# Two of eight directly transformed token tiles done by seven block products, with the weights' combinations prepared earlier

## The chip, the cores and the metric

The kernel runs on one core of one Trainium2 chip. The metric is device time in microseconds (us) of one execution. Differences of about 0.2% (1.3 us) are what a measurement of this kernel can tell from none.

## The reference, cut to what matters

```python
xn = _layernorm(x, axis=-1)                     # x: 2048 tokens x 512 channels
a = einsum("bsd,ed->bse", xn, dft_hid_re)       # DFT along the channels
b = einsum("bsd,ed->bse", xn, dft_hid_im)
s = einsum("ts,bse->bte", dft_seq_re, a) - einsum("ts,bse->bte", dft_seq_im, b)
y = _layernorm(xn)
g = silu(gelu(y @ w1 + b1) @ w2 + b2)
return x + s * g
```

The change concerns the first two products alone, the channel DFT.

## The kernel before

All matrices are float32. Each is split into a rounded high part (an fp32r copy made by ScalarE, ACT below) and a low part (value minus high part, made by VectorE, DVE below), and each product is made of three matmuls on TensorE (PE below): high x high, high x low, low x high. A matmul here takes a 128x128 stationary piece and 512 moving columns.

The program has four stages: the channel DFT (0 to 89 us of the profile), the first layer of the MLP, its second layer, and the sequence DFT. The 2048 tokens are 16 tiles of 128. In the first stage the tiles 0 to 7 are transformed directly: `dft_mm(i, m)` makes for tile i the real (m=0) or imaginary (m=1) result with 12 matmuls (4 pieces of channels, 3 terms), and `dft_out(i, m)` scales it out of PSUM on ACT and queues its store. Tiles 4 to 7 are the second token block; `xt_centre` takes the means off its two halves of channels `xtr[1, 0]` and `xtr[1, 1]` (tiles named xT), and `xt_make` splits them. Tiles 8 to 15 go by seven block products (Strassen's scheme in Winograd's form: two halves of channels, pairs of token tiles i and j, real and imaginary half of the result). `q_product(p)` makes product p for four pairs, six matmuls each. Its left sides are `W` (the DFT matrix itself, products 1, 2, 4) or the combinations that `a_sum`, `a_round` and `a_rest` make of it (A5, A6, A7, A3); its right sides are the halves 11, 21, 22 and the sums t1 to t4, made by `y_sum`, `y_round`, `y_rest` after `y_centre` (means) and `y_scale` (row factors). Products 1, 6, 7 and 4 accumulate in one PSUM bank (y), 5 and 3 in another (z), 2 in a third (x). Between them `q_after` reads the bank: for 1, 5, 6, 4 a scaled copy on ACT, for 2, 3, 7 a scaled addition on DVE.

Order is written out by hand: every engine executes its instructions in the order in which the code issues them, and waits on semaphores where an operand is not there or a place not free. `turn_n` and `turn_r` turn rows of means and factors (a transpose on PE, a copy rt on ACT, a store to DRAM from ACT's queue); `row_load` brings them back, spread over all partitions, through SP's queue (tiles rown and rowR). [...]

```python
    KEY_Q = {1: "y", 6: "y", 7: "y", 4: "y", 5: "z", 3: "z", 2: "x"}
```

Of the kernel before, what the change touches and what calls it, by code (L numbers as in the profile page):

```python
# [14 lines left out]
P = 128  # L15
# [5 lines left out]
def fnet_mixer_kernel(ctx: ExitStack, tc: tile.TileContext, x, xT, ct, wt, w1, w2, b1, b2, out):  # L21
# [153 lines left out]
    def rows_turn(key, copies=1):  # L175
        st = row_st[key]
        n = st.shape[1]
        ps = bank("rp" + key)
        nc.tensor.transpose(ps[:n, :P], st, ident)
        sb = small.tile([n, P], F32, tag="rt", bufs=1, name="rt" + key)  # L180
        nc.scalar.activation(sb, ps[:n, :P], AF.Copy)
        row_d[key] = dram.tile([copies, n * P], F32, name="rd" + key)
        nc.scalar.dma_start(out=row_d[key].rearrange("r (b p) -> b r p", p=P),
                            in_=sb[:, None, :].broadcast_to([n, copies, P]))
# [148 lines left out]
    def xt_centre(b, k2):  # L333
        nc.vector.tensor_sub(xtr[b, k2], xtr[b, k2], both(mrow[b]))

    def xt_make(b, k2):
        hi, lo = split_two(xtr[b, k2], f"xt{b}_{k2}")
        for k in range(2):
            for c in range(NC):
                xt[b * NC + c, 2 * k2 + k] = (hi[:, k, c * P:(c + 1) * P], lo[:, k, c * P:(c + 1) * P])  # L340

    weights = [None] * (2 * NK)

# [27 lines left out]
    def neg_means(b, n=NC):  # L371
        nc.vector.tensor_scalar(nm[:, NEG[b] * NC:NEG[b] * NC + n], mv1[:, b * NC:b * NC + n, 0], -1.0, None,
                                op0=ALU.mult)

    def act_stats(i):
        c = i % NC
        nc.scalar.activation(junk(0), xs[i], AF.Copy, scale=-1.0 / D, accum_out=nm[:, NC + c:NC + c + 1])
        nc.scalar.activation(junk(1), xs[i], AF.Square, bias=nm[:, NC + c:NC + c + 1], accum_out=sq[:, c:c + 1])
# [117 lines left out]
    dft_mm(2, 1)  # L496
    dft_out(2, 0)

    def xt_prepare(b):
        for k in range(NK // 2):  # L500
            xt_centre(b, k)
        for k in range(NK // 2):
            xt_make(b, k)


    w1_raw, w1_op = {}, {}

    def w1_load(j):
# [48 lines left out]
    def a_sum(p):  # L557
        a11, a12, a21, a22 = (room_w[m, k2] for m in range(2) for k2 in range(2))
        if p == 5:
            nc.vector.tensor_add(a22, a21, a22)  # L560
        if p == 7:
            nc.vector.tensor_sub(a21, a11, a21)
        if p == 6:
            nc.vector.tensor_sub(a11, a22, a11)
        if p == 3:
            nc.vector.tensor_sub(a12, a12, a11)
# [12 lines left out]
    RIGHT = {1: "11", 2: "21", 3: "22", 4: "t4", 5: "t1", 6: "t2", 7: "t3"}  # L579
    KEY_Q = {1: "y", 6: "y", 7: "y", 4: "y", 5: "z", 3: "z", 2: "x"}  # L580
    qx, q_part = {}, {}

    def q_place(name, c):
        if c % 2 == 0:
            q_part[name, c] = guest(f"q{name}_{c}")
        return q_part[name, c - c % 2][:, c % 2, :]


    def q_out(i, m, e):
# [1 line left out]
        while len(stores) > LAG:  # L591
            store()

    def q_after(p, c):
        i, j = 2 * NC + c, 3 * NC + c
        f, g = (qq[:, t - HB:t - HB + 1] for t in (i, j))
        nf, ng = (nq[:, t - HB:t - HB + 1] for t in (i, j))
        acc = qx[KEY_Q[p], c]
        if p in (1, 5, 6, 4):
            e = q_place(p, c)  # L600
            nc.scalar.activation(e, acc, AF.Copy, scale={1: f, 5: ng, 6: g, 4: nf}[p])
            if p == 4:
                q_out(i, 1, e)
        else:
            e = q_part[{2: 1, 3: 6, 7: 5}[p], c - c % 2][:, c % 2, :]
            nc.vector.scalar_tensor_tensor(e, acc, {2: f, 3: g, 7: ng}[p], e, op0=ALU.mult, op1=ALU.add)
            q_out(*{2: (i, 0), 3: (j, 0), 7: (j, 1)}[p], e)

    def q_mm(p, c):
        key = KEY_Q[p]  # L610
        yh, yl = y_op[RIGHT[p], 1]
        if p in (1, 5, 2):
            qx[key, c] = bank(f"q{key}{c}")
        cols = slice(c * P, (c + 1) * P)
        terms = [(a[:, k, cols], w) for k in range(2)
                 for a, w in ((yh, a_op[p][k][0]), (yh, a_op[p][k][1]), (yl, a_op[p][k][0]))]
        for n, (a, w) in enumerate(terms):
            nc.tensor.matmul(qx[key, c], a, w, start=p in (1, 5, 2) and n == 0,  # L618
                             stop=p in (2, 3, 4) and n == len(terms) - 1, skip_group_check=True)

    def q_product(p, *steps):
        for c in range(NC):
# [3 lines left out]
            for do in steps[c:c + 1]:  # L626
                for o in do:
                    o()

    def turn_n():  # L630
        row_st["n"] = nm
        rows_turn("n")
        mrow[2], mrow[3] = row_load("n", 2)

    def turn_r():
        row_st["R"] = rr[:, HB:3 * HB]
        rows_turn("R")

    for i in range(3, HB):
        if i == 3:  # L640
            xt_prepare(1)
            for q in (13, 14, 15):
                act_stats(q)
            for q in (10, 11):
                stats(mv1, xs[q], q)
            neg_means(2)
            neg_means(0, 2)
        if i == 4:
            factors = second_factors()
            a_sum(5)  # L650
            factors()
        if i == 5:
            a_sum(7)
            last_factors()
            a_sum(6)
            a_sum(3)
        if i == 6:
            for b in (2, 3):
                for k2 in range(2):
                    y_centre(b, k2)  # L660
        if i == 7:
            y_scale(0, 2)
            y_round("11", 1)
            y_scale(1, 2)
            y_round("21", 1)
            y_rest("11", 1)
            y_rest("21", 1)
        dft_mm(i, 0, {4: turn_r} if i == 5 else {})
        if i == 5:
            rrow = [None] * 2 + row_load("R", 2, 2)  # L670
        dft_out(i - 1, 1)
        dft_mm(i, 1, {3: turn_n} if i == 4 else {})
        dft_out(i, 0)
    dft_out(HB - 1, 1)

    for p, (m, k2) in {1: (0, 0), 2: (0, 1), 4: (1, 1)}.items():
        a_op[p] = [weights[m * NK + 2 * k2 + k] for k in range(2)]
# [4 lines left out]
    def then(f, *a):  # L682
        return lambda: f(*a)

    rrow[0:2] = row_load("R", 2)
    centred_load(0)
    y_scale(0, 3)
    a_round(5)
    y_sum("t1", 1)
    y_round("t1", 1)  # L690
    a_rest(5)
    y_rest("t1", 1)
    q_product(1, [then(y_scale, 1, 3), then(y_round, "22", 1)], [then(y_sum, "t2", 1)],
              [then(y_round, "t2", 1), then(y_rest, "22", 1)], [then(a_round, 6)])
    q_product(2, [post(2, 0), then(y_rest, "t2", 1)], [post(2, 1), then(a_rest, 6)],
              [post(2, 2), then(y_sum, "t3", 1), then(y_round, "t3", 1), then(a_round, 3)], [post(2, 3)])
    q_product(5, [then(a_rest, 3)], [then(y_rest, "t3", 1), then(y_sum, "t4", 1), then(a_round, 7)],
              [then(y_round, "t4", 1), then(a_rest, 7)], [then(y_rest, "t4", 1)])
    early.close()
    wr = early.enter_context(tc.tile_pool(name="wr", bufs=1, reuse_waits="tile"))  # L700
    wp = early.enter_context(tc.tile_pool(name="wp", bufs=4, reuse_waits="tile"))
# [454 lines left out]
    def factors(u, name):  # L1156
        q, n = units[u]
        lr = [[t[:, (n % 2) * W2 + k * P:(n % 2) * W2 + (k + 1) * P] for k in range(2)] for t in c_left[q, n // 2][name]]
        return lr, c_ops[u][name]
# [154 lines left out]
```

## Time and profile before

| | |
|---|---|
| median of 3 runs | 666.75 us (666.4 to 666.99) |
| profiled execution, its own time | 666.61 us |
| its span | 664.8 us |
| PE busy | 659.8 us (99%), 2920 matmuls |
| DVE busy | 538.9 us (81%) |
| ACT busy | 359.8 us (54%) |
| granted TensorE clock | 1.00 in every stretch |

The span runs from the first instruction to the last. The profiled execution's own time is 1.8 us more than its span and 0.14 us under the median.

### The profile page before, as it was taken

Reading aid. Unit: us, or ns where it says so; the run is one execution under the profiler, and the core shown is the slowest. Engines: PE = TensorE matmul, PEld = TensorE weight load, DVE = VectorE, ACT = ScalarE, POOL = GpSimd, SP = SyncE. Lnnn points to the kernel's source line nnn. Section 1 sums busy time; section 2 is a strip of 40 time slices with the busy share of each in tenths; the row PEclk is TensorE's granted clock in tenths of the full one; section 3 lists DMA queues with packets and bytes.
Section 4 is the critical chain, followed back from the end, with each engine's and each line's share of the span. In section 5 each row is a group of like instructions: output and inputs, shape, how many; then the busy total and the mean of one; then the engine's idle time right before and its main releaser. Section 6 shows DMA issues by size and latency. Waiting matters only on the chain.

```text
span 664.8 us, 8196 instructions
## 1 busy us (share of the span) xinstructions
PE 659.8 (99%) x2920; PEld 543.8 (82%) x2920; DVE 538.9 (81%) x570; ACT 359.8 (54%) x413; POOL 50.8 (8%) x84
## 2 busy tenths in 40 slices
PE   9999999999999999999999999999999999999997
PEld 5888888888888888888888888888888888888886
DVE  7789978866777866888979998739877299997986
ACT  6846557545456755555455544456444454646540
POOL 0002000321121100000000000000000001210100
PEclk9999999999999999999999999999999999999999
DMA  9889250887979999798699996416545558996984
GB/s 316 276 278 253 92 227 1 331 310 277 340 299 353 416 413 365 268 387 311 254 389 409 373 321 228 159 51 203 188 149 134 128 131 263 301 258 238 317 253 139
DMA packets 71877, 172.81 MB, mean 260 GB/s; under 512 B 6896, under 2 KB 22812, under 8 KB 71836
## 3 DMA queue, kind: packets, MB, share of 16 engines
q1 hardware_dynamic: 59488, 132.27, 56.6%
q0 software_dynamic: 12032, 39.86, 18.9%
q8 instruction: 23, 0.38, 0.2%
q10 hardware_dynamic: 316, 0.16, 0.1%
q14 instruction: 18, 0.15, 0.1%
HBM read 121.91 MB, written 50.35 MB: 259 GB/s over the span
## 4 chain that ended last, share of the span: by engine, by line
PE 99%; DVE 0%; issue 0%
PE pz L928 20%; PE px L928 18%; PE ma L928 11%; PE hy L743 11%; PE mb L928 9%; PE hz L743 6%; PE pd L397 5%; PE pw L928 5%; PE qy L618 3%; PE hx L743 3%; PE pd L409 2%; PE px L1249 2%; PE pw L1249 2%; PE qz L618 2%; PE qx L618 1%; PE idle_ps L202 1%
## 5 line engine op out<-in xcount | busy, mean ns | idle before, releaser
L1034 DVE TENSOR_TENSOR c<-c,c 128x1024 f32<-128x1024 f32 x32 | 39.0, 1217 | 4.2 <-DMA c<-ct 4.2
L81 DVE TENSOR_TENSOR w1l<-w1r,w1h 128x1792 fp32r<-128x1792 f32 x7 | 14.2, 2025 | 21.6 <-ACT w1h L521 21.6
L748 ACT ACTIVATE hc<-hc,b_t 128x1024 f32<-128x1024 f32 (+1 forms) x18 | 17.3, 961 | 25.0 <-DVE hc L788 22.6
L63 DVE TENSOR_TENSOR R_b1l<-c,R_b1h 128x1024 fp32r<-128x1024 f32 x16 | 19.4, 1220 | 12.9 <-ACT R_b1h L62 9.9
L62 ACT ACTIVATE R_s3h<-c 128x1024 fp32r<-128x1024 f32 x16 | 17.0, 1062 | 23.7 <-DVE c L1034 9.5
L928 PE MATMUL pw<-R_s1h,L 128*128 128x512 f32 x96 | 29.7, 389 | 0.0
L62 ACT ACTIVATE R_b2h<-c 128x1024 fp32r<-128x1024 f32 x16 | 16.9, 1057 | 21.2 <-DVE c L1039 15.0
L63 DVE TENSOR_TENSOR R_s2l<-c,R_s2h 128x1024 fp32r<-128x1024 f32 x16 | 19.5, 1220 | 8.6 <-PE pz L928 8.6
L62 ACT ACTIVATE R_s2h<-c 128x1024 fp32r<-128x1024 f32 x16 | 17.0, 1061 | 16.7 <-PE px L928 9.3
L62 ACT ACTIVATE R_s1h<-c 128x1024 fp32r<-128x1024 f32 x16 | 16.4, 1050 | 11.7 <-DVE c L1045 11.7
L63 DVE TENSOR_TENSOR R_s3l<-c,R_s3h 128x1024 fp32r<-128x1024 f32 x16 | 19.5, 1218 | 4.0 <-PE pz L928 4.0
L1042 POOL DMA_DIRECT2D c<-ct x8 | 7.0, 873 | 200.8 <-DVE c L1039 162.9
L62 ACT ACTIVATE R_b1h<-c 128x1024 fp32r<-128x1024 f32 x16 | 16.7, 1053 | 10.4 <-DMA c<-ct 4.4
L62 ACT ACTIVATE R_a1h<-c 128x1024 fp32r<-128x1024 f32 x16 | 16.9, 1054 | 8.9 <-PE pz L928 7.2
L928 PEld LDWEIGHTS pw<-R_s1h,L 128*128 128x128 f32 x96 | 18.0, 188 | 3.7
L63 DVE TENSOR_TENSOR R_b2l<-c,R_b2h 128x1024 fp32r<-128x1024 f32 x16 | 19.4, 1217 | 1.9 <-PE px L928 1.9
L63 DVE TENSOR_TENSOR R_a1l<-c,R_a1h 128x1024 fp32r<-128x1024 f32 x16 | 19.5, 1218 | 1.3 <-PE px L928 1.1
L62 ACT ACTIVATE R_s4h<-c 128x1024 fp32r<-128x1024 f32 x16 | 16.8, 1049 | 6.1 <-PE pz L928 3.3
L63 DVE TENSOR_TENSOR R_s4l<-c,R_s4h 128x1024 fp32r<-128x1024 f32 x16 | 19.5, 1218 | 0.7 <-PE px L928 0.7
L1039 DVE TENSOR_TENSOR c<-c,c 128x1024 f32<-128x1024 f32 x16 | 19.6, 1222 | 0.4
L62 ACT ACTIVATE w2h<-w 128x1024 fp32r<-128x1024 f32 (+1 forms) x14 | 13.2, 944 | 10.7 <-DVE w L856 3.9
L63 DVE TENSOR_TENSOR R_s1l<-c,R_s1h 128x1024 fp32r<-128x1024 f32 x16 | 18.8, 1219 | 0.1
(968 smaller groups left out, 2221.6 us busy)
## 6 DMA issues: line engine op xcount, KB each, us to landing
c<-ct SPq DMA_DIRECT2D x68, 512.0 KB, 5.6
m<-h_d SPq DMA_DIRECT2D x48, 512.0 KB, 7.0
h_d<-ht POOLq DMA_DIRECT2D x21, 512.0 KB, 7.0
s_d<-sa SPq DMA_DIRECT2D x32, 256.0 KB, 4.0
la<-s_d SPq DMA_DIRECT2D x32, 256.0 KB, 6.7
h_d<-hc POOLq DMA_DIRECT2D x13, 512.0 KB, 3.8
x<-x SPq DMA_DIRECT2D x16, 256.0 KB, 5.2
sa<-a_d SPq DMA_DIRECT2D x8, 512.0 KB, 5.8
```

What stands on the lines that cost most here:

```text
L62: nc.scalar.activation(hi, src, AF.Copy)
L63: nc.vector.tensor_sub(lo, src, hi.bitcast(F32))
L81: nc.vector.tensor_sub(hi_lo[1], src, hi_lo[0].bitcast(F32))
L397: nc.tensor.matmul(acc, xt[i, k][px], weights[m * NK + k][pw], start=n == 0, stop=n == len(terms) - 1)
L409: nc.tensor.matmul(dacc[i, m], xt[i, k][px], weights[m * NK + k][pw], start=seen[i, m] == 0, stop=seen[i, m] == 3 * NK - 1)
L618: nc.tensor.matmul(qx[key, c], a, w, start=p in (1, 5, 2) and n == 0, stop=p in (2, 3, 4) and n == len(terms) - 1, skip_group_check=True)
L743: nc.tensor.matmul(acc[:, tau, :], w[:, W1_AT[p], k * P:(k + 1) * P], r[:, k, :], start=p in (1, 5, 2) and i == 0, stop=p in (2, 3, 4) and ...
L748: nc.scalar.activation(dst, src, AF.Gelu_apprx_tanh, bias=b1_t[:, row:row + 1])
L928: nc.tensor.matmul(acc[k][:, tau, :], a, c[:, tau, :], start=first and i == 0, stop=last and i == len(terms) - 1, skip_group_check=True)
L1034: nc.vector.tensor_sub(t, t, raw)
L1039: nc.vector.tensor_add(raw, raw, t)
L1249: nc.tensor.matmul(acc[KEY[name]][k][:, tau, cols], a[k], c[:, tau, cols], start=False, stop=last and u == us[-1] and i == 2, skip_group_c ...
```

## The change

Tiles 6 and 7, the last two of the second token block, no longer go through `dft_mm`. They become one pair of the seven block products, taken on the centred columns, with results scaled by the row factors `rr` and `nr1` (`tau` = "u"). Tiles 4 and 5 stay direct; `xt_round` splits their columns only. Sums t1 to t4, high and low parts of the pair are 2x128 columns wide. `a_sum`, `a_round` and `a_rest` move ahead of the products of the pair; means and factors of tiles 8 to 15 (`y_centre`, `y_scale`) move behind them, between the products. The turned rows get two places (rt) in place of one.

```diff
-        sb = small.tile([n, P], F32, tag="rt", bufs=1, name="rt" + key)
+        sb = small.tile([n, P], F32, tag="rt", bufs=2, name="rt" + key)
...
+    PAIRS = 1
+    CONV = NC - 2 * PAIRS
+    half_ops = {}
+
+    def xt_round(b, k2):
+        n = CONV * P
+        if k2 == 0:
+            half_ops[b] = operand(f"xt{b}h"), operand(f"xt{b}l")
+        hi, lo = (t[:, :, k2 * n:(k2 + 1) * n] for t in half_ops[b])
...
+        nc.scalar.activation(hi, xtr[b, k2][:, :, :n], AF.Copy)
+        return lambda: nc.vector.tensor_sub(lo, xtr[b, k2][:, :, :n], hi.bitcast(F32))
...
     def y_round(name, tau):
+        if tau == "u":
+            y_op[name, tau] = u_place(name)
+            nc.scalar.activation(y_op[name, tau][0], y_raw[name, tau], AF.Copy)
+            return
...
+    def q_scale(tau, t):
+        if tau == 1:
+            return qq[:, t - HB:t - HB + 1], nq[:, t - HB:t - HB + 1]
+        return rr[:, t:t + 1], nr1[:, t:t + 1]
...
+    def u_product(p):
+        for c in range(PAIRS):
+            q_mm(p, c, "u")
+            if p in (1, 5, 6, 4):
+                q_after(p, c, "u")
+
+    def u_after(p):
+        for c in range(PAIRS):
+            q_after(p, c, "u")
...
-    for i in range(3, HB):
...
+    def u_make(name):
+        y_sum(name, "u")
+        y_round(name, "u")
+
+    a_sum(5)
+    for k2 in range(2):
+        xt_centre(1, k2)
...
+    a_sum(7)
+    dft_mm(3, 0)
+    dft_mm(3, 1)
+    factors = second_factors()
+    a_sum(6)
+    factors()
+    a_sum(3)
+    dft_mm(4, 0)
+    dft_mm(4, 1, {3: turn_n})
+    dft_out(2, 1)
+    dft_out(3, 0)
+    a_round(5)
+    y_rest("11", "u")
+    u_make("t1")
+    dft_out(3, 1)
+    a_rest(5)
+    y_rest("t1", "u")
+    dft_mm(5, 0, {4: turn_r})
+    rrow = [None] * 2 + row_load("R", 2, 2)
+    a_round(6)
+    u_make("t2")
+    dft_out(4, 0)
+    a_rest(6)
+    y_rest("t2", "u")
+    dft_mm(5, 1)
+    y_round("21", "u")
+    y_rest("21", "u")
+    a_round(7)
+    u_make("t3")
+    dft_out(4, 1)
+    a_rest(7)
...
+    a_round(3)
...
+    u_product(1)
+    dft_out(5, 0)
+    u_product(5)
+    dft_out(5, 1)
+    u_make("t4")
+    y_rest("t4", "u")
+    u_product(6)
+    y_centre(2, 0)
+    y_scale(0, 2)
+    y_round("11", 1)
+    u_product(2)
+    last_factors()
+    u_after(2)
+    u_product(7)
+    u_after(7)
+    u_product(3)
+    u_product(4)
+    y_rest("11", 1)
+    y_centre(2, 1)
+    y_scale(1, 2)
+    y_round("21", 1)
+    u_after(3)
+    y_rest("21", 1)
...
+    q_product(1, [then(y_centre, 3, 0), then(y_scale, 0, 3)], [then(y_sum, "t1", 1)],
+              [then(y_round, "t1", 1)], [then(y_centre, 3, 1)])
+    q_product(2, [then(y_rest, "t1", 1), post(2, 0)], [then(y_scale, 1, 3), then(y_round, "22", 1), post(2, 1)],
+              [then(y_sum, "t2", 1), then(y_round, "t2", 1), post(2, 2)], [post(2, 3), then(y_rest, "22", 1)])
```

On ACT, from the copy of the turned factors (rtR) on, before: `e` are the scaled results of `dft_out`, `y11_1h` is a high part for tiles 8 to 15.

```order
L181 ACTIVATE rtR_540<-rpR_538 16x128
L183 DMA rdR_542<-rtR_540 16x128
L420 ACTIVATE e4_524<-pd4_1_503,nr1_86 128x512
L420 ACTIVATE e5_569<-pd5_0_533,rr_85 128x512
L420 ACTIVATE e5_569<-pd5_1_556,nr1_86 128x512
L420 ACTIVATE e6_604<-pd6_0_576,rr_85 128x512
L77 ACTIVATE y11_1h_608<-xT2_0_397 128x1024
```

And in the change: `A6h`, `A7h`, `A3h` are the high parts of the weights' combinations, `uh0` and `uh1` hold high parts of the pair, `qu1_0<-quy0` is the copy of product 1 of the pair.

```order
L181 ACTIVATE rtR_543<-rpR_541 16x128
L183 DMA rdR_545<-rtR_543 16x128
L77 ACTIVATE A6h_557<-rw00_110 128x1024
L563 ACTIVATE uh0_430<-xT1_0_258 128x2x128
L429 ACTIVATE e4_562<-pd4_0_487,rr_85 128x512
L563 ACTIVATE uh0_430<-xT1_1_260 128x2x128
L77 ACTIVATE A7h_582<-rw10_117 128x1024
L563 ACTIVATE uh1_586<-xT1_0_258 128x2x128
L429 ACTIVATE e4_562<-pd4_1_500,nr1_86 128x512
L563 ACTIVATE uh1_586<-xT1_1_260 128x2x128
L77 ACTIVATE A3h_594<-rw01_113 128x1024
L635 ACTIVATE qu1_0_606<-quy0_599,rr_85 128x512
```

The high parts of t2, 21, t3 and 22 and of three of the weights' combinations now stand between the turned factors and the copy of product 1, with the two results of tile 4 among them.

On DVE, before, around the first use of the rows (`rown` means, `rowR` factors):

```order
L535 TENSOR_TENSOR xT2_0_397<-xT2_0_397,rown_0_513 128x1024
L535 TENSOR_TENSOR xT2_1_399<-xT2_1_399,rown_0_513 128x1024
L535 TENSOR_TENSOR xT3_0_401<-xT3_0_401,rown_0_513 128x1024
L535 TENSOR_TENSOR xT3_1_403<-xT3_1_403,rown_0_513 128x1024
L538 TENSOR_TENSOR xT2_0_397<-xT2_0_397,rowR_2_552 128x1024
L538 TENSOR_TENSOR xT2_1_399<-xT2_1_399,rowR_2_552 128x1024
```

And in the change (`ul1` is the low part of t4, `qq` and `nq` come of `last_factors`, the two rows on `qu1_0` are `u_after(2)` and `u_after(7)`):

```order
L575 TENSOR_TENSOR xT1_0_258<-xT1_1_260,xT1_0_258 128x2x128
L81 TENSOR_TENSOR ul1_587<-xT1_0_258,uh1_586 128x2x128
L537 TENSOR_TENSOR xT2_0_397<-xT2_0_397,rown_0_510 128x1024
L540 TENSOR_TENSOR xT2_0_397<-xT2_0_397,rowR_2_555 128x1024
L160 TENSOR_TENSOR qq_88<-vv_87,rr_85 128x8
L161 TENSOR_TENSOR qq_88<-qq_88,rr_85 128x8
L162 TENSOR_SCALAR nq_89<-qq_88 128x8
L640 SCALAR_TENSOR_TENSOR qu1_0_606<-qux0_637,rr_85,qu1_0_606 128x512
L640 SCALAR_TENSOR_TENSOR qu1_0_606<-quy0_599,nr1_86,qu1_0_606 128x512
L81 TENSOR_TENSOR y11_1l_635<-xT2_0_397,y11_1h_634 128x1024
L537 TENSOR_TENSOR xT2_1_399<-xT2_1_399,rown_0_510 128x1024
L540 TENSOR_TENSOR xT2_1_399<-xT2_1_399,rowR_2_555 128x1024
```

One `y_centre`, one `y_scale` and `last_factors` now stand between the low part of t4 and the two additions; the other `y_centre` are spread behind.

## Rows read from the trace of the kernel before

**Rows 1.** Busy time by engine (the page's first part), and PE's waits.
```profile
PE 659.8 (99%) x2920; PEld 543.8 (82%) x2920; DVE 538.9 (81%) x570; ACT 359.8 (54%) x413; POOL 50.8 (8%) x84
...
PE idle_ps L202 <- DVE warm L237: 1.2, 1, 1.2
```

**Rows 2.** Chain that ended last: start us, length us, engine, tile, line, instructions.
```profile
51.50 5.44 PE qy L618 x24
...
62.38 5.44 PE qz L618 x24
...
649.90 11.13 PE px L1249 x66
```

**Rows 3.** Windows, us: busy PE, PEld, DVE, ACT, POOL, clock, DMA share, GB/s.
```profile
36.00:44.00 8.00, 8.00 (x37) 6.61 (x36) 4.88 (x6) 2.85 (x5) 0.00 (x0) 1.00 0.58 171
44.00:52.00 8.00, 8.00 (x37) 6.62 (x36) 7.96 (x8) 3.81 (x6) 0.00 (x0) 1.00 1.02 356
```

**Rows 4.** Timeline of ACT: start us, length us, instruction, xcount [idle before].
```profile
5.91 0.38 ACT L62 ACTIVATE xt<-pt 128x256 fp32r<-128x256 f32 x1
6.19 0.62 ACT L347 ACTIVATE W<-rw 128x512 fp32r<-128x512 f32 x1
...
22.64 0.69 ACT L420 ACTIVATE e<-pd,rr 128x512 f32<-128x512 f32 x1 [1.14 <-DVE mv L117]
23.22 0.68 ACT L420 ACTIVATE e<-pd,nr 128x512 f32<-128x512 f32 x1
...
37.96 0.27 ACT L181 ACTIVATE rtR<-rpR 16x128 f32<-16x128 f32 x1 [2.41 <-PE pd L397]
...
38.66 0.69 ACT L420 ACTIVATE e<-pd,nr 128x512 f32<-128x512 f32 x1 [0.43 <-ACT rtR L181]
...
66.12 1.04 ACT L77 ACTIVATE A3h<-rw 128x1024 fp32r<-128x1024 f32 x1
67.07 1.25 ACT L601 ACTIVATE q<-qz,nq 128x512 f32<-128x512 f32 x2
```

**Rows 5.** Timeline of DVE, 24 to 75 us.
```profile
24.66 2.36 DVE L334 TENSOR_TENSOR xT<-xT,rowm 128x1024 f32<-128x1024 f32 x2 [1.40 <-DMA rowm<-rdm]
...
32.53 0.17 DVE L138 TENSOR_SCALAR vv<-sq 128x4 f32<-128x4 f32 x1 [1.19 <-ACT squares L378]
...
35.81 0.16 DVE L160 TENSOR_TENSOR qq<-vv,rr 128x8 f32<-128x8 f32 x1
...
36.29 1.22 DVE L564 TENSOR_TENSOR rw<-rw,rw 128x1024 f32<-128x1024 f32 x1
...
41.80 4.63 DVE L535 TENSOR_TENSOR xT<-xT,rown 128x1024 f32<-128x1024 f32 x4 [3.04 <-DMA rown<-rdn]
46.47 2.36 DVE L538 TENSOR_TENSOR xT<-xT,rowR 128x1024 f32<-128x1024 f32 x2
...
51.11 1.22 DVE L538 TENSOR_TENSOR xT<-xT,rowR 128x1024 f32<-128x1024 f32 x1
52.36 1.23 DVE L552 TENSOR_TENSOR xT<-xT,xT 128x1024 f32<-128x1024 f32 x1
...
59.39 0.75 DVE L606 SCALAR_TENSOR_TENSOR q<-qx,qq,q 128x512 f32<-128x512 f32 x1
...
61.45 0.74 DVE L606 SCALAR_TENSOR_TENSOR q<-qx,qq,q 128x512 f32<-128x512 f32 x1
62.11 1.22 DVE L81 TENSOR_TENSOR A6l<-rw,A6h 128x1024 fp32r<-128x1024 f32 x1
...
74.09 0.42 DVE L514 TENSOR_TENSOR w1r<-w1r 128x256 f32<-128x256 f32 x1
74.43 0.42 DVE L515 TENSOR_TENSOR w1r<-w1r 128x256 f32<-128x256 f32 x1
```

**Rows 6.** The tile rowR: its loads on SP's queue, and issue to landing.
```profile
L190 SPq DMA_DIRECT2D rowR<-rdR x2: 319/462/605, 41.9 to 47.2; - x2
...
DMA to landing us min/median/max: 4.5/5.1/5.8
```

More of the change, by code (lines that the diff above doesn't have):

```diff
@@ L334, in xt_centre @@
         nc.vector.tensor_sub(xtr[b, k2], xtr[b, k2], both(mrow[b]))
-    def xt_make(b, k2):
-        hi, lo = split_two(xtr[b, k2], f"xt{b}_{k2}")
+    PAIRS = 1
[6 more added lines that the diff above has]
+        hi, lo = (t[:, :, k2 * n:(k2 + 1) * n] for t in half_ops[b])
         for k in range(2):
-            for c in range(NC):
+            for c in range(CONV):
                 xt[b * NC + c, 2 * k2 + k] = (hi[:, k, c * P:(c + 1) * P], lo[:, k, c * P:(c + 1) * P])
+        nc.scalar.activation(hi, xtr[b, k2][:, :, :n], AF.Copy)
+        return lambda: nc.vector.tensor_sub(lo, xtr[b, k2][:, :, :n], hi.bitcast(F32))
     weights = [None] * (2 * NK)
@@ L497, in fnet_mixer_kernel @@
     dft_out(2, 0)
[L499 to L503, printed above, removed]
     w1_raw, w1_op = {}, {}
@@ L539, in y_scale, with u_place, u_parts @@
         y_raw[f"{k2 + 1}{b % 2 + 1}", b // 2] = xtr[b, k2]
+    U_ORDER = ("11", "t1", "t2", "21", "t3", "22", "t4")
+    u_tiles = {}
+    def u_place(name):
+        w = PAIRS * P
+        n, at = divmod(U_ORDER.index(name), W // w)
+        if n not in u_tiles:
+            u_tiles[n] = operand(f"uh{n}"), operand(f"ul{n}")
+        return [t[:, :, at * w:(at + 1) * w] for t in u_tiles[n]]
+    def u_parts():
+        w = PAIRS * P
+        for k2 in range(2):
+            for h in range(2):
+                at = CONV * P + h * w
+                y_raw[f"{k2 + 1}{h + 1}", "u"] = xtr[1, k2][:, :, at:at + w]
     def y_round(name, tau):
+        if tau == "u":
+            y_op[name, tau] = u_place(name)
+            nc.scalar.activation(y_op[name, tau][0], y_raw[name, tau], AF.Copy)
+            return
         y_op[name, tau] = rounded(y_raw[name, tau], f"y{name}_{tau}")
@@ L581, in fnet_mixer_kernel, with q_at, q_place @@
     qx, q_part = {}, {}
[L583 to L586, printed above, removed]
+    Q_TILES = {1: lambda c: (2 * NC + c, 3 * NC + c), "u": lambda c: (NC + CONV + c, NC + CONV + PAIRS + c)}
+    def q_scale(tau, t):
+        if tau == 1:
+            return qq[:, t - HB:t - HB + 1], nq[:, t - HB:t - HB + 1]
+        return rr[:, t:t + 1], nr1[:, t:t + 1]
+    def q_at(tau, name, c):
+        if tau == "u" and PAIRS == 1:
+            return (tau, name in (1, 5)), int(name in (5, 4))
+        return (tau, name, c // 2), c % 2
+    def q_place(tau, name, c):
+        key, at = q_at(tau, name, c)
+        if key not in q_part:
+            q_part[key] = guest(f"q{tau}{name}_{c}")
+        return q_part[key][:, at, :]
     def q_out(i, m, e):
@@ L592, in q_out, with q_after @@
             store()
[L594 to L598, printed above, removed]
+    def q_after(p, c, tau=1):
+        i, j = Q_TILES[tau](c)
+        (f, nf), (g, ng) = q_scale(tau, i), q_scale(tau, j)
+        acc = qx[tau, KEY_Q[p], c]
         if p in (1, 5, 6, 4):
-            e = q_place(p, c)
+            e = q_place(tau, p, c)
             nc.scalar.activation(e, acc, AF.Copy, scale={1: f, 5: ng, 6: g, 4: nf}[p])
@@ L604, in q_after, with q_mm @@
         else:
-            e = q_part[{2: 1, 3: 6, 7: 5}[p], c - c % 2][:, c % 2, :]
+            e = q_place(tau, {2: 1, 3: 6, 7: 5}[p], c)
             nc.vector.scalar_tensor_tensor(e, acc, {2: f, 3: g, 7: ng}[p], e, op0=ALU.mult, op1=ALU.add)
             q_out(*{2: (i, 0), 3: (j, 0), 7: (j, 1)}[p], e)
-    def q_mm(p, c):
-        key = KEY_Q[p]
-        yh, yl = y_op[RIGHT[p], 1]
+    def q_mm(p, c, tau=1):
+        key = tau, KEY_Q[p], c
+        yh, yl = y_op[RIGHT[p], tau]
         if p in (1, 5, 2):
-            qx[key, c] = bank(f"q{key}{c}")
+            qx[key] = bank(f"q{tau}{KEY_Q[p]}{c}")
         cols = slice(c * P, (c + 1) * P)
@@ L617, in q_mm @@
         for n, (a, w) in enumerate(terms):
-            nc.tensor.matmul(qx[key, c], a, w, start=p in (1, 5, 2) and n == 0,
+            nc.tensor.matmul(qx[key], a, w, start=p in (1, 5, 2) and n == 0,
                              stop=p in (2, 3, 4) and n == len(terms) - 1, skip_group_check=True)
@@ L637, in turn_r @@
         rows_turn("R")
-    for i in range(3, HB):
[L640 to L674, printed above, removed]
     for p, (m, k2) in {1: (0, 0), 2: (0, 1), 4: (1, 1)}.items():
@@ L683, in then @@
         return lambda: f(*a)
+    def u_make(name):
+        y_sum(name, "u")
+        y_round(name, "u")
+    a_sum(5)
+    for k2 in range(2):
+        xt_centre(1, k2)
+    rests = [xt_round(1, k2) for k2 in range(2)] if CONV else []
+    for o in rests:
+        o()
+    u_parts()
+    y_round("11", "u")
+    for q in (13, 14, 15):
+        act_stats(q)
+    for q in (10, 11):
+        stats(mv1, xs[q], q)
+    neg_means(2)
+    neg_means(0, 2)
+    a_sum(7)
+    dft_mm(3, 0)
+    dft_mm(3, 1)
@@ new lines, in fnet_mixer_kernel @@
+    a_round(7)
+    u_make("t3")
+    dft_out(4, 1)
+    a_rest(7)
+    y_rest("t3", "u")
+    y_round("22", "u")
+    a_round(3)
+    y_rest("22", "u")
+    a_rest(3)
+    u_product(1)
[16 more added lines that the diff above has]
+    y_rest("11", 1)
@@ L685, in fnet_mixer_kernel @@
+    y_centre(2, 1)
[3 more added lines that the diff above has]
+    y_rest("21", 1)
     rrow[0:2] = row_load("R", 2)
     centred_load(0)
[L687 to L696, printed above, removed]
@@ L697, in fnet_mixer_kernel @@
-    q_product(5, [then(a_rest, 3)], [then(y_rest, "t3", 1), then(y_sum, "t4", 1), then(a_round, 7)],
-              [then(y_round, "t4", 1), then(a_rest, 7)], [then(y_rest, "t4", 1)])
+    q_product(1, [then(y_centre, 3, 0), then(y_scale, 0, 3)], [then(y_sum, "t1", 1)],
+              [then(y_round, "t1", 1)], [then(y_centre, 3, 1)])
+    q_product(2, [then(y_rest, "t1", 1), post(2, 0)], [then(y_scale, 1, 3), then(y_round, "22", 1), post(2, 1)],
+              [then(y_sum, "t2", 1), then(y_round, "t2", 1), post(2, 2)], [post(2, 3), then(y_rest, "22", 1)])
@@ L699, in fnet_mixer_kernel @@
+    q_product(5, [then(y_rest, "t2", 1)], [then(y_sum, "t3", 1), then(y_round, "t3", 1)],
+              [then(y_sum, "t4", 1), then(y_rest, "t3", 1)], [then(y_round, "t4", 1), then(y_rest, "t4", 1)])
     early.close()
```

## Prediction

> **What bounds the kernel now.** The page's busy times come first [rows 1]: PE is busy 99% of the span, and the view of waits names a single wait of PE, 1.2 us at its very start. The reader should see in it that no other engine costs anything today; every wait of DVE and ACT lies beside PE's work. The chain of waits then gives PE's pace: 24 matmuls in 5.44 us, so 0.2267 us each [rows 2], the same in the early stage as later, and the clock is 1.00 in each window [rows 3]. So PE's count sets the time as long as everything PE needs is there, and the question is whether that lasts. The windows show how full the helpers are where the change works: ACT 2.85 and DVE 4.88 of 8 us from 36 to 44, ACT 3.81 and DVE 7.96 of 8 from 44 to 52 [rows 3]. DVE has no room in the second. The timelines of ACT and DVE [rows 4, 5] then give the intervals from which its new queue can be added up.
>
> **What is removed on PE.** Two tiles by 24 matmuls are 48; seven products by six are 42. Six fewer at 0.2267 save 1.36 us. [...]
>
> **What needs no more.** `a_sum(5)` on DVE goes into the 1.40 us in which DVE waited for the means' row [rows 5]; at 1.14 it fits, and past that gap it would push `xt_centre` and with it tile 4. The second place for turned rows lets rtR be copied without the earlier store being done; before, ACT stood 2.41 us ahead of it [rows 4]. Nothing on the new path waits for that, so I cost it at nothing. The weights' rounds and rests are the same work, moved.
>
> **What it costs, first wait.** Intervals from start to start: an ACT result of 512 columns 0.58 (22.64 to 23.22), an ACT round of 1024 0.95 (66.12 to 67.07), rtR with its DMA issue 0.70 (37.96 to 38.66) [rows 4]; a DVE operation of 1024 columns 1.14, or 1.25 where the next needs its result (51.11 to 52.36, so a release takes 0.03) [rows 5]. The 2x128 operations of the pair do not occur; the nearest rows are of 256 columns, ACT 0.28 (0.38 to its end) [rows 4] and DVE 0.34 (0.42 to its end) [rows 5]. I take these. Below, they could be a quarter of the 1024 operation, 0.24 and 0.28; above, the full 0.38 and 0.42 with no overlap.
>
> The clock starts at 32.53 on DVE, when ACT's last square is in; that stays, since ACT's list before it is about as long. Until 35.81 [rows 5] the same five small operations and two weight sums run, 6 and 3 in place of 5 and 7. Then the rest of 11 (0.34, end 36.23) and t1's sum (36.26 to 36.68). ACT goes on from 36.71: t1 0.28, a result of tile 3 0.58, rtR 0.70, so A6h begins at 38.27 and ends 1.04 later. DVE can then make A6's rest from 39.34 (1.14), two low parts (0.34 each) and t3's sum (to 41.58). Meanwhile ACT has done t2, a result, 21 and A7h, is free at 41.31 and waits to 41.61 for t3. Then t3 0.28, a result 0.58, 22 0.28, A3h 0.95 and the copy of product 1, 0.69: it ends at 44.39, and PE may go on at 44.42.
>
> PE wants it sooner. Today it starts the seven products of tiles 8 to 15 at 51.50 [rows 2]; tile 6 starts 48 matmuls earlier, at 40.62. The pair's products 1 and 5 take 12 matmuls, to 43.34. Product 6 accumulates in the bank that the copy of product 1 still reads. **Wait 1: 44.42 - 43.34 = 1.08 us.** Behind it PE's whole queue stands.
>
> **Second wait.** Product 4 takes the same bank again and needs `u_after(7)` on DVE. ACT goes on from 43.70 + 0.58 = 44.28 with two results and the copy of product 5, 0.58 each, so t4's round runs 46.02 to 46.40. DVE: t4's rest from 46.43 (0.34), `y_centre` 1.25, `y_scale` 1.14, `last_factors` 0.48 (35.81 to 36.29), `u_after(2)` 0.66 (61.45 to 62.11), `u_after(7)` 0.74 to its end [rows 5]: 51.04, PE 51.07. After wait 1, PE reaches product 4 after 24 more matmuls, at 49.86. **Wait 2: 1.21 us.** The 1.25 + 1.14 of row work ahead of the two additions is what makes it. (Product 7, before that, needs the copy of product 6, on ACT from 46.30 to 46.99; PE asks at 47.14, so it is free by 0.15.)
>
> **Third place.** Product 5 of tiles 8 to 15 needs the banks of product 2, which DVE reads. Before, the first addition ended at 60.14 [rows 5] and the z stretch of PE's chain begins at 62.38 [rows 2], two microseconds later. Before, too, the four `y_centre` ran at 41.80 to 46.4; now they stand between the additions. From 50.96 DVE runs: rest 1.14, centre 1.25, scale 1.14, addition 0.66 (to 55.15), a wait for ACT's round of 21 to 55.69, rest 1.14, centre 1.25, scale 1.25, sum 1.14, centre 1.14, a wait of 0.06, rest 1.14 (to 62.81), and the first addition ends at 63.55. PE: 51.07 + 30 x 0.2267 + 24 x 0.2267 = 63.31. That is 0.27 of waiting. Each of the next two banks has one 1024 operation and one addition before it, 1.14 + 0.66 = 1.80, against six matmuls, 1.36: 0.44 each. The fourth addition follows directly and is early. **Wait 3: 1.15 us.** Behind it DVE has to make t2, t3 and t4 with two products' time each; there I see no wait.
>
> **Sum.** 1.08 + 1.21 + 1.15 - 1.36 = +2.08 us. The profiled execution's span of 664.8 becomes 666.9 and its own time 668.7; against the median, 0.14 higher, 668.8. The bounds of the 2x128 operations move it: three ACT and three DVE of them lie on the path in series with the waits, so -0.3 at their low end and +0.5 at their high end.
>
> [...] The rows show 0.38 in length, but only 0.28 before the next may start, so I stay with that.
>
> **Rivals.** *All hidden.* ACT has the copy of product 1 done by 43.34, DVE the addition 7 by 48.78, and the banks are free in time. Then only the six matmuls count: 665.4, faster. For it speaks that PE does not wait anywhere today [rows 1] and that ACT has over 5 us free from 36 to 44 [rows 3]. Against it: the seven rounds and three of the weights' go into just that stretch, and the list is in order; the copy would have to be 1.08 earlier, and 2.29 would have to go from DVE's list. Chance 0.05.
>
> *Half hidden.* The ACT and DVE lists are as long as I say up to product 4, but DVE catches up by the third place (the rounds it waits for come sooner, or the moved `y_centre` fit in). Then 1.08 + 1.21 - 1.36 = +0.93: 667.7, which is within 0.2%. Chance 0.13.
>
> *The row comes late.* `y_scale` stands ahead of the two additions that product 4 waits for, and it needs rowR. On SP's queue three stores, where one stood, now come between the load of rown and that of rowR. Loaded as before, at 41.9 with 4.5 us to landing [rows 6], it is there at 46.4, and `y_scale` asks at 48.02. If SP is blocked 1.7 longer and the load takes 5.8, as the other of the two did, it lands at 49.4, product 4 starts 1.4 later, and so does everything behind it: 670.2. Under 1.6 us of lateness it costs nothing. Chance 0.20, with any other lengthening of DVE's list.
>
> That the change does not do what it says I exclude: the order lists 42 matmuls where 48 stood.
>
> **Numbers.** Forecast 668.8 with 0.62; late row 0.20; half hidden 0.13; all hidden 0.05. The least difference that the measurement can tell from none is 0.2%, 1.33 us, so 668.08: the forecast and the late row are slower, 0.82; half hidden is the same, 0.13; all hidden, 1.36 down, is faster, 0.05. The range leaves out all hidden and the outer parts of the two others: 667.4 to 670.4.
>
> **What would show it.** In the profile after: 2914 matmuls; PE waits that are not there today, on ACT's copy of product 1 (about 1.1 us, near 44), on DVE's addition 7 (about 1.2, near 51) and on DVE at z (0.3, 0.4, 0.4, from 63 to 67); `y_scale` not waiting for DMA. PE at the pace of 0.2267 everywhere else, the first product of tiles 8 to 15 at about 52.4 where it was 51.50. It is wrong if PE shows no waits between 40 and 70, if the pair's 2x128 operations are far from 0.28 and 0.34, or if a wait appears behind 70.

## The result and the profile after

The changed kernel takes **668.82 us** (median of 7 runs, 668.64 to 669.49), the kernel before in the same measurement 666.58 us (7 runs, 666.23 to 666.99). The ratio is 1.0035, 95% interval 1.0023 to 1.0046: slower by 2.2 us, and by more than the 0.2% that can be told from none. The forecast was 668.8, slower. The profiled execution of the change took 668.77 us with a span of 667.0, against 664.8 before.

The busy times and PE's waits, to be held against [rows 1]:

```profile
PE 659.8 (99%) x2914; PEld 542.1 (81%) x2914; DVE 543.8 (82%) x584; ACT 361.4 (54%) x420; POOL 50.7 (8%) x84
```

```profile
PE idle_ps L202 <- DVE warm L237: 1.2, 1, 1.2
PE quy L652 <- DVE qu L640: 1.0, 1, 1.0
PE quy L652 <- ACT qu L635: 0.9, 1, 0.9
```

PE has its six matmuls fewer and yet the same 659.8 us of busy time and the same 99%. The share of busy time tells nothing here; the two new lines of the view of waits do. The windows say where (busy PE, PEld, DVE, ACT, POOL, clock, DMA share, GB/s), to be held against [rows 3]:

```profile
36.00:44.00 8.00, 7.24 (x32) 5.63 (x30) 6.73 (x12) 7.06 (x14) 0.00 (x0) 1.00 0.63 191
44.00:52.00 8.00, 6.87 (x29) 5.38 (x30) 6.85 (x12) 3.77 (x7) 0.00 (x0) 1.00 1.03 356
...
60.00:68.00 8.00, 7.65 (x32) 5.42 (x31) 7.96 (x10) 4.33 (x6) 1.37 (x3) 1.00 1.05 257
68.00:76.00 8.00, 8.00 (x37) 6.61 (x36) 7.12 (x7) 5.47 (x8) 0.00 (x0) 1.00 0.17 65
```

From 36 to 44 ACT went from 2.85 to 7.06 of 8 us, and PE lost 0.76. From 44 to 52 PE lost 1.13 while DVE, at 6.85, was not even full: it stood in its own list waiting for ACT (1.05 us for t4's round, shown in experiment 2). From 60 to 68 DVE is full (7.96) and PE lost 0.35. Behind 68 PE is whole again. The clock is 1.00 throughout.

PE's own timeline at the three places (start us, length us, tile, shape, [idle before and what ended it]):

```profile
42.85 0.39 PE L652 MATMUL quz<-A5h,ul 128*128 128x512 f32 x1
44.15 0.50 PE L652 MATMUL quy<-A6h,uh 128*128 128x512 f32 x1 [0.91 <-ACT qu L635]
44.48 0.39 PE L652 MATMUL quy<-A6l,uh 128*128 128x512 f32 x1
...
49.49 0.39 PE L652 MATMUL quz<-A3h,ul 128*128 128x512 f32 x1
50.86 0.74 PE L652 MATMUL quy<-W,uh 128*128 128x512 f32 x2 [0.98 <-DVE qu L640]
...
63.05 0.39 PE L652 MATMUL q1x<-W,y_1l 128*128 128x512 f32 x1
63.55 0.47 PE L652 MATMUL q1z<-A5h,yt_1h 128*128 128x512 f32 x1
...
64.78 0.39 PE L652 MATMUL q1z<-A5h,yt_1l 128*128 128x512 f32 x1
65.25 0.50 PE L652 MATMUL q1z<-A5h,yt_1h 128*128 128x512 f32 x1
...
66.51 0.40 PE L652 MATMUL q1z<-A5h,yt_1l 128*128 128x512 f32 x1
67.05 0.50 PE L652 MATMUL q1z<-A5h,yt_1h 128*128 128x512 f32 x1
```

What a wait costs is read from start to start, not from the idle time in brackets: 42.85 to 44.15 is 1.30 where 0.227 is the pace, so 1.07 lost at product 6 (the bracket says 0.91, since a matmul's 0.39 overlaps the next). At product 4 it is 1.37 - 0.23 = 1.14, at z 0.27, 0.24 and 0.31, which stand in no line of waits, since the overlap leaves at most 0.15 of each idle. The sum is 3.0. And behind each wait there is a second, small loss: the first matmul takes 0.47 to 0.50 instead of 0.39, and the next starts 0.31 to 0.34 later (44.15 to 44.48) instead of 0.227. Five times 0.1 is 0.5. With 3.0 + 0.5 - 1.36 the account stands at 2.2. The spans differ by 2.2, and the stretch compared below by 2.34; the missing 0.14 are matmuls that start 0.23 to 0.24 apart for a while behind a wait. The account also says why the busy time stayed: per wait 0.16 is covered by the matmul that still runs and 0.1 is the slower restart, five times 0.26, nearly as much as the six matmuls.

### The profile page after: what moved, and what is told of

Read it like the earlier page. It is cut to its first block, busy times and chain, and to the rows that moved or that the text cites. A ratio compares the mean times of both kernels' runs of the same rounds, so it can differ in the third digit from the quotient of the medians.

```text
span 667.0 us, 8210 instructions
## 1 busy us (share of the span) xinstructions
PE 659.8 (99%) x2914; PEld 542.1 (81%) x2914; DVE 543.8 (82%) x584; ACT 361.4 (54%) x420; POOL 50.7 (8%) x84
## 4 chain that ended last, share of the span: by engine, by line
PE 92%; DVE 3%; DMA 2%; ACT 2%; issue 1%; ACTq 0%; SPq 0%; DVEq 0%
PE pz L1007 20%; PE px L1007 18%; PE hy L822 11%; PE ma L1007 11%; PE mb L1007 9%; PE hz L822 6%; PE pw L1007 5%; PE hx L822 3%; PE q1y L652 2%; PE pd L418 2%; PE px L1328 2%; PE pw L1328 2%; PE q1z L652 1%; DMA w1r<-w 1%; PE idle_ps L202 1%
```

## The experiments

The start of a program scatters: PE's short waits in its first 10 us differ from execution to execution (its first eleven direct matmuls begin at 5.97 us before, at 5.70 in the change), and its turn of the factors (rpR) falls between 35.28 and 36.54 in the profiles. So beside the medians, one stretch of each profiled execution is compared that leaves this out: from rpR to the last stage's matmuls (px). PE's timeline before and in the change, and the end of the chain in the change:

```profile
35.78 0.27 PE L179 MATMUL rpR<-ident,rr 128*16 128x128 f32 x1
...
62.22 0.39 PE L618 MATMUL qz<-A5h,yt_1h 128*128 128x512 f32 x1
```

```profile
35.69 0.27 PE L179 MATMUL rpR<-ident,rr 128*16 128x128 f32 x1
```

```profile
652.15 11.13 PE px L1328 x66
```

Before, this is 649.90 [rows 2] - 35.78 = 614.12, in the change 616.46.

| run | median, us | runs | ratio to before, 95% interval | stretch against before |
|---|---|---|---|---|
| the change | 668.82 | 7 | 1.0035 (1.0023 to 1.0046) | +2.34 |
| one place for turned rows | 668.93 | 4 | 1.0037 (1.0024 to 1.0051) | +2.54 |
| copy of product 1 earlier | 669.05 | 5 | 1.0039 (1.0026 to 1.0052) | +2.82 |
| row work into DVE's gap | 667.72 | 11 | 1.0020 (1.0011 to 1.0029) | +1.26 |
| order alone | 667.34 | 11 | 1.0015 (1.0006 to 1.0024) | +0.83 |
| before less six matmuls | 665.83 | 11 | 0.9991 (0.9983 to 1.0000) | -0.98 |
| order and ACT copies | 665.59 | 11 | 0.9991 (0.9982 to 1.0000) | -0.89 |

The kernel before ran beside them 21 times in each of two measurements, with medians of 666.53 and, for the two rows with "order" in the name, 666.41.

**Theory:** PE's waits are set by two hand-written lists, ACT's up to the copies and DVE's up to the additions, and they stand in series: a wait that is removed at one place turns up at the next, as long as DVE's list ends no sooner. **Rival:** each wait costs by itself, and what is removed is gained. **Second rival:** the block products as such cost too much (small operations, more evictions), whatever their order.

**1. The first wait alone.** Product 1 is issued ahead of two rounds, so ACT copies its bank sooner:

```diff
     y_rest("t3", "u")
+    u_product(1)
     y_round("22", "u")
     a_round(3)
     y_rest("22", "u")
     a_rest(3)
-    u_product(1)
     dft_out(5, 0)
```

> From the change: product 1 of the pair is issued ahead of the rounds of 22 and A3, so ACT copies its bank before them. The queue theory (the waits stand in series behind one list on DVE): product 6 waits no more (its 1.07 us near 44 goes), but ACT's list up to the copy of product 6 has the same members, so that copy still ends near 46.9 and product 7 waits for it about 1.0 us; t4's round and with it DVE's addition 7, which ends at 50.80 in the change, do not move. Time as the change, 668.8, within 0.3 us. The rival (each wait costs by itself, and one removed is gained): 1.07 us less, or 1.2 with the slower first matmul behind it, 667.6.

Measured: 669.05, no gain. PE's timeline and DVE's of this kernel:

```profile
42.45 0.39 PE L652 MATMUL quz<-A5h,ul 128*128 128x512 f32 x1
42.98 0.50 PE L652 MATMUL quy<-A6h,uh 128*128 128x512 f32 x1
...
45.62 0.39 PE L652 MATMUL qux<-W,ul 128*128 128x512 f32 x1
46.85 0.50 PE L652 MATMUL quy<-A7h,uh 128*128 128x512 f32 x1 [0.85 <-ACT qu L635]
...
50.92 0.72 PE L652 MATMUL quy<-W,uh 128*128 128x512 f32 x2 [1.02 <-DVE qu L640]
```

```profile
50.13 0.74 DVE L640 SCALAR_TENSOR_TENSOR qu<-quy,nr,qu 128x512 f32<-128x512 f32 x1
```

The wait at product 6 falls from 1.07 to 0.30, and one of 1.00 appears at product 7, which did not wait before: the copy of product 6 is still the last of ACT's list. (The expectation had no wait at product 6. PE came 0.4 us earlier in this execution, with rpR at 35.28 where the change has 35.69, while the lists of ACT and DVE were 0.1 later; that makes the 0.30, and most of what the stretch in the table is longer.) Product 4 starts at 50.92, as good as where it did (50.86), because addition 7 still begins at 50.13 (50.06 in the change). The waits are in series, and the rival is out. The wait at product 4 is the one that counts for both.

**2. The second wait alone.** The last factors and one subtraction of means go where DVE stood idle:

```diff
     u_make("t4")
+    last_factors()
+    y_centre(2, 0)
     y_rest("t4", "u")
     u_product(6)
-    y_centre(2, 0)
     y_scale(0, 2)
...
-    last_factors()
     u_after(2)
```

> From the change: the last factors and the first subtraction of means of tiles 8 to 15 stand ahead of the low part of t4 on DVE, where DVE stood idle 1.05 us for t4's round. The queue theory: addition 7 ends some 1.05 us sooner, at about 49.7, product 4 waits for at most 0.2 us instead of 1.14, and since all of DVE's later list comes as much sooner, the three waits at z stay 0.2 to 0.3 each; wait 1 is as before. 667.6, that is 1.0 to 1.3 less than the change. Rival one (DVE has too much work from 50 to 66, its order in front does not count): what wait 2 gives back is taken at z, 668.8. Rival two (the factors' row comes late): the scaling asks for rowR at about 47.1 instead of 47.76 and waits for its DMA; then half is lost, 668.2.

Measured: 667.72, 1.1 less than the change. DVE of the change, and then of this kernel, up to addition 7:

```profile
46.17 0.43 DVE L81 TENSOR_TENSOR ul<-xT,uh 128x256 fp32r<-128x256 f32 x1 [1.05 <-ACT uh L563]
46.51 1.22 DVE L537 TENSOR_TENSOR xT<-xT,rown 128x1024 f32<-128x1024 f32 x1
47.76 1.22 DVE L540 TENSOR_TENSOR xT<-xT,rowR 128x1024 f32<-128x1024 f32 x1
...
50.06 0.74 DVE L640 SCALAR_TENSOR_TENSOR qu<-quy,nr,qu 128x512 f32<-128x512 f32 x1
```

```profile
45.85 1.23 DVE L537 TENSOR_TENSOR xT<-xT,rown 128x1024 f32<-128x1024 f32 x1
46.99 0.42 DVE L81 TENSOR_TENSOR ul<-xT,uh 128x256 fp32r<-128x256 f32 x1
47.32 1.22 DVE L540 TENSOR_TENSOR xT<-xT,rowR 128x1024 f32<-128x1024 f32 x1
...
49.12 0.74 DVE L640 SCALAR_TENSOR_TENSOR qu<-quy,nr,qu 128x512 f32<-128x512 f32 x1
```

The subtraction fills the gap of 1.05, addition 7 begins 0.94 sooner, and product 4 follows product 3 without a wait (49.83 to 50.07 in PE's timeline). The three waits at z keep their sum, only sooner: from the first product of tiles 8 to 15 to the third bank at z it is 66.11 - 51.44 = 14.67 us, in the change 67.05 - 52.37 = 14.68. Wait 1 is there as before, 1.27 in this execution. The interval of the ratio overlaps that of the change; what settles it is that the stretch is 1.08 shorter and that the wait at product 4 is gone from the timeline. Rival one is out, since the waits at z did not grow. The scaling at 47.32 follows the operation before it, so the factors' row was there.

**3. What six matmuls are worth before.** In the kernel before, six of the twelve matmuls of tile 7's imaginary result are left out:

```diff
+        if (i, m) == (7, 1):
+            terms = terms[:6]
```

> The kernel before with six of the twelve matmuls of tile 7's imaginary result left out (half of its terms are missing); everything else as it was. It asks what six matmuls are worth there. Theory: PE comes to z 1.36 us sooner, but DVE's third and fourth additions end at 63.98 and 65.78 as before, while PE would ask for their banks at 63.58 and 64.94 plus the first wait; so it waits some 0.4 and 0.3 us and twice 0.1 behind that, and only 0.4 to 0.6 of the 1.36 comes out: 666.1. The rival (PE's count alone sets the time): 1.36 less, 665.2.

Measured: 0.70 less than before, 665.83, with the runs spread from 665.37 to 666.67; the interval takes in no change and a gain of 1.1, not the 1.36. Half came out in the median, a little more than the 0.4 to 0.6 expected, and the profiled execution shows less waiting than I had worked out: a single gap at z.

```profile
64.71 0.40 PE L620 MATMUL qz<-A5h,yt_1l 128*128 128x512 f32 x1
65.16 0.50 PE L620 MATMUL qz<-A5h,yt_1h 128*128 128x512 f32 x1
65.49 0.39 PE L620 MATMUL qz<-A5l,yt_1h 128*128 128x512 f32 x1
```

That is 0.22 and then 0.11, where I had 0.4, 0.3 and twice 0.1. In this execution DVE's work on the means' row began at 41.26, not 41.80 [rows 5], and all additions came 0.67 sooner, 0.54 of it from there. Both times DVE stood idle until that row landed (3.04 us in [rows 5], 2.35 in this execution), so the landing sets the start of DVE's list in this kernel. That it differs from execution to execution, and so makes the spread of 1.3 us, is argued from these two profiles, not shown.

**4. The second place for turned rows.** One place again:

```diff
-        sb = small.tile([n, P], F32, tag="rt", bufs=2, name="rt" + key)
+        sb = small.tile([n, P], F32, tag="rt", bufs=1, name="rt" + key)
```

> The change with one place for the turned rows, as before. My reading, that the second place changes nothing: ACT's copy of the turned factors waited before for PE's transpose, not for the earlier store; 668.8 within 0.3 us. The rival (the place held it): the copy goes from 37.28 back to 37.96, all of ACT's list behind it is 0.7 us later, and so is the copy of product 1: 669.5.

Measured: 668.93, no change. The copy rtR starts at 37.52 where the change has 37.28, and the operations in front of it are as much later, so the place does not hold it here: it starts 0.57 behind the result ahead of it, as in the change (36.95 and 36.71), with no idle time named. But my reading of the kernel before, that the copy waited for PE's transpose, is wrong. There the transpose began at 35.78 and took 0.27, and the copy came only at 37.96, 0.07 behind the load of rown (37.89). The profile puts that wait down to PE [rows 4]; in the execution of experiment 3, which has the same code up to here, the profile names the store:

```profile
37.41 0.27 ACT L181 ACTIVATE rtR<-rpR 16x128 f32<-16x128 f32 x1 [1.73 <-DMA rdn<-rtn]
```

So one place did hold the copy before the change, and there it cost PE nothing. In the change ACT comes to the copy when the store has landed (rown's load, which needs it, was issued at 35.69, the copy began at 37.28), with one place or two.

**5. The order alone, and 6. the order with three additions taken off PE's path.** The two kernels share the order (the expectation of 5 lists it). Its core:

```diff
     y_rest("22", "u")
+    y_rest("t4", "u")
+    u_product(5)
     a_rest(3)
-    u_product(1)
-    dft_out(5, 0)
-    u_product(5)
-    dft_out(5, 1)
-    u_make("t4")
-    y_rest("t4", "u")
-    u_product(6)
     y_centre(2, 0)
     y_scale(0, 2)
-    y_round("11", 1)
+    u_product(6)
+    dft_out(4, 1)
+    dft_out(5, 0)
     u_product(2)
-    last_factors()
     u_after(2)
+    last_factors()
     u_product(7)
     u_after(7)
+    y_round("11", 1)
+    dft_out(5, 1)
```

In 6, for product 7 of the pair and for the first two pairs of product 2 of tiles 8 to 15, the addition is split in two; `late` runs when DVE has room:

```diff
+            if (p, c, tau) in SOFT:
...
+                nc.scalar.activation(s, acc, AF.Copy, scale={2: f, 3: g, 7: ng}[p])
+
+                def late():
+                    nc.vector.tensor_add(e, e, s)
```

> The block products of the change with another order alone: t1's sum and round earlier, product 1 ahead of A3's round, t4 made before product 5, the first subtraction of means of tiles 8 to 15 ahead of product 6, the last factors between the two additions, results of tiles 3 to 5 written later on ACT, each addition of product 2 at z ahead of the scaling and sums that stood before it. Queue theory: wait 1 goes, product 7 finds the copy of product 6 done, but addition 7 still stands behind a subtraction, a scaling and an addition on DVE (A3's rest near 45.4, then 1.25 + 1.14 + 0.66 + 0.48 + 0.74 = 4.3 us, so near 49.6), and PE is at product 4 at 48.5: a wait of about 1.0. At z one wait of 0.2 to 0.3 stays. 1.36 less, 1.0 + 0.3 and three times 0.1 more: 0.2 to 0.6 above the kernel before, 667.0. The rival (order is all of it, so that this hides everything): 665.2.

> The same order, and three of DVE's additions no longer stand between PE and a bank: product 7 of the pair and the first two of product 2 at z are read out of PSUM by a scaled copy on ACT (0.58 each, ACT is free there), and DVE adds the copy to the result later, when nobody waits. Queue theory: product 4 of the pair waits for nothing, at z the first bank is late by at most 0.2, so 1.36 less and 0 to 0.3 more: 1.1 to 1.3 under the kernel before, 665.3. Rival one (DVE's load as such binds, since the additions are only moved): the wait comes back behind 68, where DVE makes t2 to t4 and the second bank's additions, 666.3. Rival two (the block products cost PE more than their count): 666.5 or more.

Measured: 667.34 for the order alone, 0.9 above before (0.2 to 0.6 was expected), and 665.59 with the copies, **0.8 under before** (1.1 to 1.3 was expected) and 3.2 under the change. The order alone leaves the wait that the theory names, 1.16 instead of 1.0, and one that I had not named, up to 85.43, where product 4 of tiles 8 to 15 waits for its addition 7 (in the chain DVE's additions run from 82.00 to 85.39, and PE goes on at 85.43). The only line in its view of PE's waits beside that of the program's start:

```profile
PE quy L652 <- DVE qu L640: 1.0, 1, 1.0
```

With the copies no line of PE's waits is left but the one at the program's start. PE, ACT and DVE of that kernel at product 4, PE also at its turn of the factors and at z:

```profile
35.54 0.27 PE L179 MATMUL rpR<-ident,rr 128*16 128x128 f32 x1
...
48.15 0.39 PE L666 MATMUL quz<-A3h,ul 128*128 128x512 f32 x1
48.37 0.62 PE L666 MATMUL quy<-W,uh 128*128 128x512 f32 x2
...
60.52 0.39 PE L666 MATMUL q1x<-W,y_1l 128*128 128x512 f32 x1
60.85 0.50 PE L666 MATMUL q1z<-A5h,yt_1h 128*128 128x512 f32 x1
61.19 0.40 PE L666 MATMUL q1z<-A5l,yt_1h 128*128 128x512 f32 x1
```

```profile
47.21 0.69 ACT L647 ACTIVATE qsu<-quy,nr 128x512 f32<-128x512 f32 x1 [0.88 <-PE quy L666]
```

```profile
53.08 0.68 DVE L650 TENSOR_TENSOR qu<-qu,qsu 128x512 f32<-128x512 f32 x1
```

ACT, idle 0.88 before it, reads the bank as soon as product 7 is done, and has done so at 47.90; product 4 starts at 48.37, in step. DVE makes the addition only at 53.08, 4.7 us behind product 4's start, and nobody waits for it. Behind 68 no wait of more than 0.06 comes back (from product 6 of tiles 8 to 15 to px the chain takes 648.77 - 66.63 = 582.14 us, before 649.90 - 67.82 = 582.08), so DVE's load as such does not bind. With the same 42 matmuls the block products now lose nothing, and the second rival is out, too. Of the 1.36 some 0.9 remains in the compared stretch (a gap of 0.10 at z and 0.11 for the restart behind it, and a few slower matmuls). The gain of 0.8 over the kernel before is under the 0.2% that can be told, and the interval of 0.9982 to 1.0000 has its upper end at no change, so that this kernel is faster is likely but not shown; the gain over the change is not in doubt. Three additions were moved at once; what each is worth alone was not tried.

## Why the prediction was right

**The saving.** Six matmuls at 0.2267 are confirmed by the last experiment: from rpR to the first matmul at z it is 62.22 - 35.78 = 26.44 us before and 60.85 - 35.54 = 25.31 there, 1.13 less, and of the missing 0.23 the gap at z is 0.10 and one matmul that starts late, at 50.50, 0.08. In experiment 3, too, the stretch is 0.98 shorter with 0.33 of waiting and restart in it.

**First wait.** Predicted 1.08, measured 1.07. The mechanism was right, but that the two agree to 0.01 is luck. The prediction took 51.50 from the chain as the start of the first product of tiles 8 to 15 [rows 2]; the chain counts a step from the end of the matmul before it. In PE's timeline of the kernel before, that product starts at 51.34:

```profile
51.34 0.62 PE L618 MATMUL qy<-W,y_1h 128*128 128x512 f32 x2
```

So PE was to ask at 43.18, not 43.34, and the wait on paper was 1.24. In the change PE asked at 43.08 and got on at 44.15 (44.42 predicted), because DVE's step at which the prediction's clock starts came at 32.19 in this execution, not at 32.53, and ACT's list came 0.3 sooner with it. In experiments 2 and 4 the same lists came 0.35 and 0.24 later (A7's rest at 41.50 for 41.15, rtR at 37.52 for 37.28), and the wait is longer: from start to start 1.27 in experiment 2, and 1.1 in the view of waits of both, where the change has 0.9. The releaser is the copy of product 1, at the end of this ACT list:

```profile
42.47 1.05 ACT L77 ACTIVATE A3h<-rw 128x1024 fp32r<-128x1024 f32 x1
43.42 0.67 ACT L635 ACTIVATE qu<-quy,rr 128x512 f32<-128x512 f32 x1
...
45.70 0.44 ACT L563 ACTIVATE uh<-xT 128x256 fp32r<-128x256 f32 x1
46.01 0.71 ACT L635 ACTIVATE qu<-quy,rr 128x512 f32<-128x512 f32 x1
```

**Second wait.** Predicted 1.21, measured 1.14: addition 7 ended at 50.80 (51.04 predicted), and the second experiment shows that it is the row work ahead of the additions, as the step said. **Third place.** The kernel's pool of these banks has eight places (`bufs=8`), which products 1 and 2 of four pairs fill, so product 5 takes those of product 2. Predicted 0.27 + 0.44 + 0.44 = 1.15, measured 0.27 + 0.24 + 0.31 = 0.82, and 0.3 for the slow restarts. The first matmul there came at 63.55 (63.58 predicted), and DVE's additions follow 1.79 apart (1.80 predicted):

```profile
62.66 0.75 DVE L640 SCALAR_TENSOR_TENSOR q<-q1x,qq,q 128x512 f32<-128x512 f32 x1
...
64.45 0.75 DVE L640 SCALAR_TENSOR_TENSOR q<-q1x,qq,q 128x512 f32<-128x512 f32 x1
...
66.24 1.41 DVE L640 SCALAR_TENSOR_TENSOR q<-q1x,qq,q 128x512 f32<-128x512 f32 x2
```

**No price** stood for the restart behind a wait: five times 0.1, the one term that was missing. It hardly shows in the sum, because a wait ends when the bank's reader is done, whatever PE did before (product 4 started 0.06 us behind the end of addition 7 in the change, 0.05 in experiment 1): a PE that is later by a restart waits that much less at the next bank, which is most of why the waits at z were 0.33 smaller than I had them. At the end of the chain the change is 2.25 later (652.15 against 649.90), where 2.08 was predicted: the third bank at z came 0.13 sooner than on paper (67.05 against 63.58 + 2 x 1.80), the last restart and slower matmuls behind it added 0.14, and the start misread by 0.16 had made the sum that much too small.

**The 2x128 operations.** ACT's are 0.40 to 0.44 long and 0.30 to 0.33 from start to start (0.28 taken), DVE's 0.42 and 0.34 (taken so). On ACT the length is not what counts: an operation that stands ready starts 0.09 to 0.13 us before the end of the 2x128 operation ahead of it (42.17 + 0.41 is 42.58, and A3's round starts at 42.47).

**The rivals.** *All hidden* and *half hidden* are wrong as to this order: the waits at z are there, and DVE does not catch up until behind 68. *The row comes late*: the scaling started at 47.76, straight behind the subtraction, so it did not wait. **What would show it** held but for two points: 2914 matmuls, waits near 44 and 51 with the named releasers and three from 63 to 67, 52.37 for the first product of tiles 8 to 15 (52.4 predicted), nothing behind 70. The waits at z are too short for the change's view of waits to name DVE (experiments 1 and 4 name it for the first), and behind each wait the pace was for a while not 0.2267. One place was as tight as foreseen: product 7 was free by 0.15 on paper, and by 0.28 in the change (the copy of product 6 ended at 46.72, PE came at 47.00), but it waits as soon as PE comes sooner (experiment 1).

## What to carry to other kernels

Six matmuls fewer, 1.36 us, were worth their time here only where each bank that PE takes again was read by then: with 3.0 us of waits the kernel was 2.2 us slower, with a single one of 0.10 (experiment 6) 0.9 us came out in the compared stretch. So for each saved matmul, look for the reader of the bank it accumulates in, and add up what stands ahead of that reader in its engine's list. The waits on these lists were in series: with most of the first removed (experiment 1) nothing was gained, with the last ahead of z removed (experiment 2) 1.1 us. So remove the last, not the first. Where an engine with room can read the bank by a plain copy (ACT's copy of product 7 took 0.69 us), the arithmetic on it may come later on the full engine; here a better order took the 2.2 us lost to 0.9, and the copies took another 1.75.

## What the runs showed of the hardware

Behind each wait of PE of 0.1 us or more that the timelines of the change and of experiments 1, 2, 3 and 6 show singly, about 0.1 us (0.08 to 0.12) was lost beyond the wait itself: the first matmul behind it took 0.47 to 0.50 us instead of 0.39, and the second started 0.31 to 0.35 us behind it instead of 0.227. It was the same behind a wait of 1.27 us (experiment 2: 0.50 and 0.34) as behind one of 0.10 (experiment 6: 0.50 and 0.34). By these figures, an estimate, five short waits cost PE 0.4 us more than one long one of the same sum, but a restart that stands ahead of another wait only makes that one shorter. The mean granted clock was 0.999 to 1.00 in every execution.
